# A rebuilt opening of a fused mLSTM-cell and tanh-shrink kernel: transfers, early gates, clock filling and the split of work between VectorE and ScalarE

## The chip, the core and the metric

The kernel runs on one core of a Trainium2 chip. The metric is the device time of one execution in microseconds (us). Before the change it is 556.27 us, the median of three runs (555.25 to 557.56).

## The reference, cut to what matters

Two blocks follow each other. The first is an mLSTM cell over 4 batches, 8 heads, 768 steps and head dimension 40; its output, turned to 3072 tokens by 320 features, goes through a two-layer MLP (320 to 2048 to 320).

```python
for t in range(S):
    m_new = np.maximum(f_gate[:, :, t] + m, i_gate[:, :, t])
    f_stab = np.exp(f_gate[:, :, t] + m - m_new)
    i_stab = np.exp(i_gate[:, :, t] - m_new)
    C = f_stab * C + i_stab * einsum('bhd,bhe->bhde', vt, kt)
    n = f_stab * n + i_stab * kt
    h_tilde = einsum('bhde,bhe->bhd', C, qt)
    denom = np.maximum(np.abs(einsum(n, qt)), 1.0)
    y[:, :, t] = sigmoid(o_gate[:, :, t]) * h_tilde / denom
x = y as (B*S, H*D)
h = x @ w_in
out = (h - np.tanh(h)) @ w_out
```

The inputs are float32; the two MLP matrices come in 64-bit floats, and the kernel makes its own float32 from their bits.

## The kernel before, in words

**Units.** The cell is cut into 24 units: chunk c of 128 steps, batch b, all 8 heads, unit n = 4c + b. For a unit TensorE (PE) forms the scores of queries and keys (`scores`, L555, tile `ps`), VectorE (DVE) masks them into `P` (L564) and scales v by the input gates into `vs` (`scaled`, L546), PE multiplies `P` with `vs` per head and, for c > 0, the carried state with the queries (`intra` L589, `inter` L580, tile `ph`), DVE forms the denominator `den`, multiplies the output gate `o` by it and the result `ys` by that (`gate`, L594), PE turns `ys` (`turn`, L623, tile `px`), and ScalarE (ACT) copies it to `xT`. The state is carried by `update` (L606, tile `pc`) and `keep_state` (L614). A float32 matmul stands in the trace as two passes.

**MLP.** Two units make a group of 256 tokens, and w_in and w_out are cut into 8 blocks p. A pair (group, p) is a first product (`up`, L751, tile `ph_up`), the shrink polynomial on ACT (`z`, `q`) and DVE (`gt`), and a second product (`down`, L806, tile `po`). The first four groups are done for p = 0, 1, 2, ... as the weights come (`RUNS`, L236). Each block is brought in by GpSimd's DMA queue (POOL) and turned from 64-bit to 32-bit floats by DVE and ACT: `parts` (two instructions), `low`, `power` (ACT), `one`, `sign`, `product` (`weights`, L450). The tiles are `w` (64-bit), `w_e`, `w_m`, `w_r`, and `w_in`, `w_out` as results.

**Gates.** `gate_rows` (L375) runs the recurrence of m along rows of 32 (batch, head); `gate_columns` (L394) turns the rows with PE, sums them with PE (`lfT` with `upto` and `ones`, tile `gate`), bounds and exponentiates them (`ei`, `inv`, `eT`). This is done in three passes, for chunk 0, chunk 1 and chunks 2 to 5 (`CHUNKS`, L365).

**What sets the order.** The first 12 units and the 32 pairs of the first four groups are planned at build time by the class `Plan` (L157): each step is put down with its engine, an assumed length, its predecessors, the buffers that it takes and gives, and a rank; `run` (L193) always takes the step that can start first, and issues its instructions. The result is a fixed list for each engine, executed in that order. The assumed lengths decide the order only. `idle` (L1099) puts matmuls of a tile of ones (`awake`, 128x512 in bf16) into stretches in which the plan leaves PE free. After the planned part (from the 32 pairs on) the order is interleaved by another piece of code.

**The opening.** Before the plan starts, the gate rows of chunks 0 and 1, `kz` of units 0 and 1 and both `o` are issued on SyncE's queue (SP), `qz` on ACT's, `v` on POOL's (L282, L316 to L321). ACT loads its table for exp when it has issued its four transfers. `qz` and `kz` hold every second head per half of the partitions, so that each of their transfers is 40 partitions of 4 pieces of 512 bytes.

Of the kernel before, what the change touches and what calls it, by code (L numbers as in the profile page):

```python
# [56 lines left out]
PSUM = bass.MemoryType.PSUM  # L57
NO_SYNC = mybir.DependencyInfo(mybir.DependencyClass.NoSync, mybir.DependencyReason.DATA)

L = 128  # L60
# [18 lines left out]
def kernel(  # L79
# [77 lines left out]
    class Plan:  # L157
# [5 lines left out]
        RATE, SHARED = 0.25, 32.4  # L163

        def __init__(self, **tokens):
            self.tokens = {name: [(0.0, tag) for tag in (range(tags) if isinstance(tags, int) else tags)] for name, tags in tokens.items()}
            self.turns = {name: 0 for name, tags in tokens.items() if isinstance(tags, int)}
            self.count = tokens
            self.todo, self.free, self.serial, self.moved = [], dict.fromkeys("TVASGN", 0.0), 0, dict(S=8.0, G=6.5)
            self.tiles = 1  # L170

        def add(self, engine, us, step, after=(), rank=0.0, take=(), give=(), at=0.0, kb=0.0, tiles=1, hold=0.0):
            self.serial += 1
            op = {"engine": engine, "us": us, "step": step, "after": list(after), "rank": rank, "serial": self.serial,
                  "take": take, "give": give, "at": at, "kb": kb, "tiles": tiles, "hold": hold, "end": None}
            self.todo.append(op)
            return op
# [15 lines left out]
        def run(self, idle):  # L193
            while self.todo:
                _, _, _, _, t, op = min(((t[1], op["engine"] == "T" and op["tiles"] != self.tiles == 2, op["rank"], op["serial"], t[0], op)
                                         for op in self.todo if (t := self.start(op)) is not None), key=lambda x: x[:4])
                self.todo.remove(op)
                for name, held in op["take"]:
                    token = self.token(name)
                    self.tokens[name].remove(token)  # L200
                    if name in self.turns:
                        self.turns[name] += 1
                    held[name] = token[1]
                if op["engine"] == "T":
                    idle(self.free["T"], t)
                    self.tiles = op["tiles"]
                op["step"]()
                op["end"] = self.free[op["engine"]] = t + op["us"]
# [69 lines left out]
    def load_gates(c0, c1):  # L278
        for to, part in ((f_sb, f_gate), (i_sb, i_gate)):
            nc.sync.dma_start(out=to[:, c0 * L:c1 * L], in_=part[:, c0 * L:c1 * L])  # L280

    load_gates(0, 2)  # L282
# [10 lines left out]
    def load_unit(n, names=("kz", "qz", "v", "k", "o", "q2"), queue=nc.sync):  # L293
        c, b = divmod(n, B)
        t = ld.setdefault(n, {})
        for name in names:
            if name in ("kz", "qz"):
                t[name] = load.tile([128, HH, L], FP, name=name, tag=name, bufs=3)
                for i in range(2):
                    src = kT if name == "kz" else qT  # L300
                    queue.dma_start(out=t[name][i * HALF:i * HALF + D], in_=src[b, c, :, slice(i, H, 2)])
# [14 lines left out]
    for n in range(2):  # L316
        load_unit(n, ("kz",))
        load_unit(n, ("qz",), A)
        load_unit(n, ("v",), G)
    for n in range(2):  # L320
        load_unit(n, ("o",))  # L321
# [5 lines left out]
    A.activation(out=probe, in_=probe, func=AF.Exp)  # L327
    ident = const.tile([128, 128], FP, name="ident")
# [6 lines left out]
    V.memset(diag, 1.0)  # L335
# [6 lines left out]
    V.memset(ones, 1.0)  # L342

# [5 lines left out]
                    pattern=[[1, 128]], channel_multiplier=-1)  # L349
    spare = []  # L350
# [14 lines left out]
    CHUNKS = (0, 1, 2, NT)  # L365
# [83 lines left out]

    def weights(dst, srcs, queue):  # L450
# [5 lines left out]
        def fetch():  # L456
# [3 lines left out]
            for rows, cols, part in srcs:  # L460
                queue.dma_start(out=to[rows, cols], in_=part)  # L461

        def parts():
# [4 lines left out]
            V.tensor_single_scalar(e, w["hi"], 0x7FF00000, op=OP.bitwise_and)  # L468
# [23 lines left out]
        return fetch, parts, low, power, one, sign, product  # L492

    def blocks_of(p):
# [4 lines left out]
        every, whole = slice(0, 128), [(slice(0, 128), slices(0, 2), moe_w_in[0:128, slices(2 * p, 2)])]  # L499
        for i in range(2):  # L500
            full, half = (FROM[2], FROM[1]), (FROM[1], FROM[2] + HALF)
            whole.append((every, slices(2 + i, 1), moe_w_in[full[i]:full[i] + 128, slices(2 * p + i, 1)]))
# [3 lines left out]
                        [(every, slice(i * DM, (i + 1) * DM), moe_w_out[slices(2 * p + i, 1), :]) for i in range(2)], nc.gpsimd))  # L506
# [29 lines left out]
    def prepare(n, whole=True):  # L536
# [4 lines left out]
        t["vs"] = scaled(n, 0, "vs", 4)  # L541
# [4 lines left out]
    def scaled(n, i, name, bufs):  # L546
# [5 lines left out]
        V.tensor_tensor(out=to[:, :, 0:D], in0=t["v"], in1=scale.unsqueeze(2).to_broadcast([L, H, D]), op=OP.mult)  # L552
# [36 lines left out]
    def intra(n, h):  # L589
        t = un[n]  # L590
        T.matmul(t["ph"][:, h, :], t["P"][:, h % 2, h // 2, :], t["vs"][:, h, :], start=(t["c"] == 0 and h == 0), stop=True,
                 skip_group_check=True)

    def gate(n):  # L594
# [4 lines left out]
        V.scalar_tensor_tensor(out=den, in0=ph[:, :, D], scalar=-1.0, in1=inv[:, t["c"], t["hs"]], op0=OP.mult, op1=OP.max)  # L599
        V.tensor_tensor(out=den, in0=den, in1=ph[:, :, D], op=OP.max)  # L600
        V.reciprocal(out=den, in_=den)
        V.tensor_tensor(out=sg, in0=sg, in1=den.unsqueeze(2).to_broadcast([L, H, D]), op=OP.mult)
        y = t["y"] = ys[n % 2]
        V.tensor_tensor(out=y.rearrange("p (h d) -> p h d", d=D), in0=ph[:, :, 0:D], in1=sg, op=OP.mult)
# [146 lines left out]
    def up(some, shrink):  # L751
# [4 lines left out]
        def product(i, x, j):  # L756
# [3 lines left out]
            if j < NK:  # L760
                lhs, rhs = w_in[:, p, (2 * j + i) * 128:(2 * j + i + 1) * 128], xT[g % NX][:, at, :]
# [110 lines left out]
    PLANNED = 12  # L872
# [60 lines left out]
    def plan_unit(n, rank):  # L933
# [10 lines left out]
        if n < 2:  # L944
            times = ((6.1, 3.6, 9.0), (7.6, 5.6, 10.5))[n]
            for name, at in zip(("qz", "v", "o"), times):
                u[name] = plan.add("N", 0.0, (lambda: arrive(n)) if name == "qz" else (lambda: None), at=at - 1.7)
        else:
            load("kz", 1.5, 164, (n - 3, "scores"))
            load("qz", 1.5, 164, (n - 3, "scores"))  # L950
            load("v", 0.5, 164, (n - 3, "prep"))
            if c:
                load("q2", 1.5, 164, (n - 3, "second"))
# [12 lines left out]
        u["scores"] = plan.add("T", 1.35, first_part, [u["qz"]], rank, [("a", held), ("P", held)], tiles=2, hold=HOLD * (n // B))  # L966
        u["mask"] = [plan.add("V", 0.68, lambda i=i: ready[1][i](), [u["scores"]], rank, give=[("a", held)] if i else ())
                     for i in range(2)]
        before = of(n - B, "state")
        u["prep"] = plan.add("V", 0.47, lambda: prepare(n, whole=False), [u["v"], u["scores"], *of_tokens[c]], rank, [("vs", held)])  # L970
        u["column"] = plan.add("A", 0.2, lambda: un[n]["column"](), [u["prep"]], rank - 0.2)
        u["open"] = plan.add("A", 0.47 if n else 1.75, lambda: open_gate(n), [u["o"], u["scores"], *of_states[0], *exponentials], rank - 0.1)
        op = None

        def second_part(j):
            banks[:] = [held["small"]]
            inter(n, j)
            for h in TRIOS[j]:
                intra(n, h)

        for j, heads in enumerate(TRIOS):
            op = plan.add("T", 0.145 * len(heads) + (0.14 if c else 0.0), lambda j=j: second_part(j), [op] if op else [*u["mask"], u["prep"], u["column"], *before, *of(n, "q2") * (c > 0)], rank,
                          take=() if op else [("small", held)], give=[("P", held)] if j == len(TRIOS) - 1 else ())
        u["second"] = op
        u["gate"] = plan.add("V", 1.5, lambda: gate(n), [op, u["open"], *of(n - 2, "turn")], rank, give=[("small", held)])
# [8 lines left out]
        def turns():  # L994
            banks[:] = [held_x["small"]]
            for j in range(NK + 1):
                turn(n, j, at_once=False)

        u["turn"] = plan.add("T", 0.35, turns, [u["gate"]], rank, [("small", held_x)])
        u["x"] = plan.add("A", 0.5, lambda: keep_x(n), [u["turn"]], rank, give=[("small", held_x)])  # L1000
        late = rank + (0.1 if c else 1.9)
        u["update"] = plan.add("T", 0.55, updates, [u["second"], u["k"]], late, [("small", held_c)], [("vs", held)],
                               at=0.0 if c else 24.0 if n < 2 else 40.0)
        u["state"] = plan.add("V", 1.0 if c else 0.5, lambda: keep_state(n), [u["update"], *before, *of_states[c]], late, give=[("small", held_c)])

    converted = {}

    def plan_weights(p, rank, at):
        for k, block in enumerate(blocks_of(p)):
            fetch, parts, low, power, one, sign, product = block  # L1010
            held, r, buffer = {}, rank + 0.36 * k, "w64" + "ab"[k]
            op = plan.add("S" if k else "G", 1.5 if k else 2.8, fetch, (), r, [(buffer, held)], at=(13.0 if p else 6.0) if k else at, kb=655)
            op = plan.add("V", 1.0, parts, [op], r, [("w", held)])
            two = [plan.add("A", 0.74, step, [op], r) for step in (low, power)]
            op = plan.add("V", 0.82, one, two[:1], r)
            op = plan.add("V", 0.82, sign, [op, two[1]], r, give=[(buffer, held)])
            converted[p, k] = plan.add("V", 0.82, product, [op] + (of_tokens[NT - 1] + of_states[NT - 1] if p >= KEPT else []), r, give=[("w", held)])

    plan.free["T"] = 2.1
    plan_gates(0, -2.0, 3.3, in_small)  # L1020
    plan_gates(1, -1.64, 3.3, in_po)
    for n in range(2):
        plan_unit(n, -1.0)
    plan_weights(0, 0.08, 3.0)
    for n in range(2, PLANNED):
        g = n // GT
        if n == 2 * B:
            plan_gates(2, 1.17, 30.0, in_po)
# [7 lines left out]
    def plan_item(x):  # L1036
# [24 lines left out]
        op = plan.add("T", 0.47 + 0.43 * n, rest, [op], rank, tiles=2)  # L1061
# [37 lines left out]
    def idle(t0, t1):  # L1099


        n = int((t1 - t0) * 0.9 / 0.43 if t0 < 6.0 else (t1 - t0) * 0.4 / 0.215)
        if n and not busy:
            awake(n)
        elif n and plan.tokens["a"] and plan.tokens["a"][0][0] <= t0:
            stream(ps_a.tile([128, 512], FP, name="awake", tag="a0"), n)

    plan.run(idle)


# [82 lines left out]
    def begin_any(n):  # L1193
# [3 lines left out]
        for i in range(2):  # L1197
            spread(t["P"][:, i], f_rows, n, slice(i, H, 2))
# [155 lines left out]
```

## Time and profile before

| | us |
|---|---|
| median of three runs | 556.27 |
| the profiled execution | 555.29 |
| its span, first to last instruction | 553.5 |
| PE busy | 538.0 (97%) |
| DVE busy | 346.2 (63%) |
| ACT busy | 182.8 (33%) |
| first `ph_up` matmul starts at | 27.44 |
| `px` of units 4, 5, 6, 7 starts at | 66.15, 76.30, 89.64, 99.92 |
| `px` of unit 11, the last planned one | 152.81 |

The profile's page gives the busy time of each engine, a picture of the span in 40 slices, the DMA queues, the chain of waits that ended last, and the costliest groups of instructions. The timeline view lists instructions in order of time and merges equal ones; "x16" are sixteen in a row. The window view gives the busy time per engine in chosen stretches. A busy PE isn't PE at its peak: `awake` matmuls count as busy, and so does a matmul that runs at half pace.

### The profile page before, as it was taken

The page shows a single profiled execution, that of the slowest core. Times are in us where ns is not written, and L with a number is a line of the kernel's source. Part 1 is how long each engine was busy: PE and PEld are TensorE (multiplying, and loading weights), DVE is VectorE, ACT ScalarE, POOL GpSimd, SP SyncE. Part 2 cuts the span into 40 slices and gives each one's busy share as a digit, 9 for nine tenths or more (in the row PEclk, how much of TensorE's full clock was granted, in tenths as well). Part 3 has the DMA queues.
Part 4 walks back from the last instruction along what each step waited for, and adds up shares of the span by engine and source line. Part 5 has one row for each costly group of instructions (what it writes and reads, how often), then busy time and mean ns, then how long its engine had stood idle before and what let it go on. Part 6 is the DMA issues. An engine that isn't in the chain of part 4 may idle for free.

```text
span 553.5 us, 8989 instructions
## 1 busy us (share of the span) xinstructions
PE 538.0 (97%) x3381; PEld 455.9 (82%) x3384; DVE 346.2 (63%) x754; ACT 182.8 (33%) x449; POOL 33.6 (6%) x67
## 2 busy tenths in 40 slices
PE   7998999999999999999999999999999999999995
PEld 5777788888877776798899999999989989988873
DVE  4699788989864335767656647547547547553421
ACT  3355734543342312322232242232233233232331
POOL 6142021400000000000000000000000000000000
PEclk9999999999999999999999999999999999999999
DMA  7798354633300001201202212112110000000000
GB/s 214 193 264 246 84 165 150 174 116 109 98 26 0 1 0 50 82 21 56 86 28 59 64 39 70 48 37 60 49 37 12 1 25 1 1 25 1 24 1 30
DMA packets 39819, 37.97 MB, mean 69 GB/s; under 512 B 3993, under 2 KB 37337, under 8 KB 39769
## 3 DMA queue, kind: packets, MB, share of 16 engines
q1 hardware_dynamic: 32336, 22.24, 14.5%
q0 software_dynamic: 3296, 10.82, 6.6%
q10 hardware_dynamic: 4136, 4.26, 2.2%
q8 instruction: 29, 0.48, 0.4%
q14 instruction: 22, 0.17, 0.1%
HBM read 33.37 MB, written 3.93 MB: 67 GB/s over the span
## 4 chain that ended last, share of the span: by engine, by line
PE 92%; DVE 3%; ACT 2%; DMA 1%; issue 1%; SPq 0%; DVEq 0%; ACTq 0%
PE ph_up L129 39%; PE pS L129 20%; PE po L129 15%; PE ph L129 9%; PE ps L129 4%; PE px L133 2%; PE pc L129 2%; DMA kz<-in_kT 1%; ACT L106 1%; DVE w_e L106 1%; DVE gt L106 1%; PE awake L129 0%; DVE P L106 0%; DVE w_in L106 0%; DVE w_r L106 0%
## 5 line engine op out<-in xcount | busy, mean ns | idle before, releaser
L129 PE MATMUL ph_up<-xT,w_in 128*128 128x256 f32 (+1 forms) x1152 | 245.9, 391 | 2.2 <-DVE w_in L106 1.1
L129 PEld LDWEIGHTS ph_up<-xT,w_in 128*128 128x128 f32 (+1 forms) x1152 | 169.4, 189 | 35.6 <-issue 13.5
L106 ACT ACTIVATE z<-ph_up 128x512 f32<-128x512 f32 (+1 forms) x100 | 57.1, 576 | 286.8 <-issue 155.6
L106 DVE SCALAR_TENSOR_TENSOR gt<-ph_up,z 128x512 f32<-128x512 f32 (+1 forms) x100 | 63.4, 663 | 92.7 <-ACT z L106 92.4
L129 PE MATMUL po<-w_out,gt 128*128 128x320 f32 x320 | 93.6, 438 | 0.8 <-ACT eT L106 0.8
L129 PEld LDWEIGHTS po<-w_out,gt 128*128 128x128 f32 x320 | 58.7, 190 | 26.1 <-issue 4.0
L106 DVE TENSOR_TENSOR P<-ps,upto 128x512 f32<-128x512 f32 x48 | 31.4, 683 | 67.5 <-PE ps L129 67.4
L106 ACT ACTIVATE q<-z,tiny 128x512 f32<-128x512 f32 (+1 forms) x100 | 64.9, 701 | 0.0
L129 PEld LDWEIGHTS ph<-vs,P 128*128 128x128 f32 x384 | 60.1, 202 | 5.7 <-issue 1.5
L106 DVE SCALAR_TENSOR_TENSOR gt<-q,gt 128x512 f32<-128x512 f32 (+1 forms) x100 | 63.1, 660 | 0.2 <-ACT q L106 0.2
L129 PE MATMUL ph<-vs,P 128*128 128x41 f32 x384 | 58.9, 273 | 0.0
L129 PE MATMUL pS<-wT,s 128*128 128x160 f32 x336 | 51.3, 300 | 0.0
L129 PEld LDWEIGHTS pS<-wT,s 128*128 128x128 f32 x336 | 47.3, 190 | 0.0
L129 PE MATMUL pS<-w_out,gt 128*128 128x160 f32 x224 | 40.4, 310 | 0.0
L129 PEld LDWEIGHTS pS<-w_out,gt 128*128 128x128 f32 x224 | 32.7, 194 | 1.3 <-issue 1.0
L129 PEld LDWEIGHTS ps<-qz,kz 40*128 40x128 f32 x384 | 27.6, 203 | 2.9 <-issue 1.2
L129 PE MATMUL ps<-qz,kz 40*128 40x128 f32 x384 | 29.1, 291 | 0.5 <-DMA kz<-in_kT 0.5
L461 POOL DMA_DIRECT2D w<-in_moe_w_in x40 | 21.7, 547 | 45.8 <-DVE w_e L106 22.3
L129 PE MATMUL ph<-state,q 120*128 120x123 f32 (+1 forms) x120 | 24.4, 284 | 0.0
L106 ACT COPY xT<-px 128x384 f32<-128x384 f32 x24 | 11.4, 474 | 33.8 <-PE px L133 33.8
L129 PEld LDWEIGHTS ph<-state,q 120*128 120x128 f32 (+1 forms) x120 | 20.0, 191 | 1.7 <-issue 0.2
L106 DVE TENSOR_TENSOR s<-gt 128x256 f32<-128x256 f32 x56 | 21.0, 416 | 0.0
(90 smaller groups left out, 445.1 us busy)
## 6 DMA issues: line engine op xcount, KB each, us to landing
w<-in_moe_w_out POOLq DMA_DIRECT2D x16, 320.0 KB, 5.2
kz<-in_kT SPq DMA_DIRECT2D x48, 80.0 KB
o<-in_o_gate SPq DMA_DIRECT2D x24, 160.0 KB
out<-ob ACTq DMA_DIRECT2D x24, 160.0 KB
k<-in_k SPq DMA_DIRECT2D x20, 180.0 KB
qz<-in_qT SPq DMA_DIRECT2D x44, 80.0 KB
v<-in_v SPq DMA_DIRECT2D x22, 160.0 KB
q<-in_qT SPq DMA_DIRECT2D x40, 60.0 KB
```

The lines of the kernel that those rows point to most:

```text
L106: i = method(*args, **kwargs)
L129: return cls.keep(nc.tensor.matmul(*args, **kwargs))
L133: return cls.keep(nc.tensor.transpose(*args, **kwargs))
L461: queue.dma_start(out=to[rows, cols], in_=part)
```

## The change

All of it lies in the opening and in the planned part.

- **Transfers.** The early ones are put in another order: `qz` of unit 0 (ACT queue), f gates, first half of `kz`, i gates, second half of `kz`; the rest of units 0 and 1 later, `v` of unit 0 on POOL between the memsets, `v` of unit 1 between two weight transfers, `o` on SP from within the plan. `qz` and `kz` now hold heads 0 to 3 and 4 to 7 per half, so that a transfer is 40 partitions of one piece of 2048 bytes. A block of weights has 4 and 1 transfers where it had 5 and 2, and the second block's first transfer waits for the first instruction that DVE runs on the first block.
- **Gates.** Chunks 0 and 1 are one pass, 256 columns wide.
- **Ones.** The tile for `awake` is set in two halves, so that its first half is ready sooner; the plan counts how dense PE's last 2.6 us were, and puts `awake` matmuls (or a dense step) before a sparse step where the share would fall under 0.48. `idle` fills 0.9 of a gap rather than 0.4, and may use any free PSUM bank.
- **ScalarE.** From unit 2 on to unit 11, the scaling of v and the product of `o` with `den` are done by ACT, head by head: 8 instructions of 128x40 each, in place of one DVE instruction of 128x320.
- **First units.** For c = 0 the product with `vs` is in two halves of four heads, each of which needs its half of the mask only.
- **Timing.** Assumed lengths, transfer rates and start times of the plan are set anew. `low` and so on are unchanged.

In program order the changed kernel has 48 `awake` matmuls (22 before), 33 of them ahead of the first `ph_up` (14 before). The tail of the PE list, from about the 32nd pair on, is the same in both.

```diff
-        RATE, SHARED = 0.25, 32.4
+        RATE, SHARED, COLD, TURN, WAIT = 0.3, 28.0, (7.0, 1.8), 0.12, 0.2
+        FEW, SPAN = 0.48, 2.6
...
+        def run(self, idle, fill):
...
+                if op["engine"] == "T":
+                    turn = self.TURN * (op["tiles"] != self.tiles)
+                    if t > self.COLD[0] and op["dense"] < 0.6 and self.share(t, op["us"], op["dense"]) < self.FEW:
+                        other = min(((x, o) for (x, _), o in ready if o["engine"] == "T" and o["dense"] >= 0.6 and x < t + 0.3),
+                                    key=lambda x: (x[1]["rank"], x[0], x[1]["serial"]), default=None)
+                        if other:
+                            t, op = other
+                        else:
+                            free = self.free["T"]
+                            n = fill(free, t + 0.3)
...
-                    queue.dma_start(out=t[name][i * HALF:i * HALF + D], in_=src[b, c, :, slice(i, H, 2)])
+                    queue.dma_start(out=t[name][i * HALF:i * HALF + D], in_=src[b, c, :, i * HH:(i + 1) * HH])
...
-    for n in range(2):
-        load_unit(n, ("kz",))
-        load_unit(n, ("qz",), A)
-        load_unit(n, ("v",), G)
-    for n in range(2):
-        load_unit(n, ("o",))
+    load_unit(0, ("qz",), A)
+    load_gates(0, 2, ((f_sb, f_gate),))
+    load_unit(0, ("kz",), between=lambda: load_gates(0, 2, ((i_sb, i_gate),)))
...
+    load_unit(1, ("kz",))
+    load_unit(1, ("qz",), A)
...
-    V.memset(diag, 1.0)
+    V.memset(diag[:, 0:HH], 1.0)
...
+    V.memset(diag[:, HH:H], 1.0)
...
-    CHUNKS = (0, 1, 2, NT)
+    CHUNKS = (0, 2, NT)
...
+                i = queue.dma_start(out=view, in_=part)
+                if behind:
+                    tc.add_manual_dep(i.ins, behind[-1].ins.name, SYNC, reason="order of transfers")
...
+        if by_heads:
+            for h in range(H):
+                A.mul(out=to[:, h, 0:D], in_=t["v"][:, h], mul=scale[:, h:h + 1])
+        else:
+            V.tensor_tensor(out=to[:, :, 0:D], in0=t["v"], in1=scale.unsqueeze(2).to_broadcast([L, H, D]), op=OP.mult)
...
+        def shares():
+            for h in range(H):
+                A.mul(out=sg[:, h], in_=sg[:, h], mul=den[:, h:h + 1])
...
-    PLANNED = 12
+    PLANNED, SHARED = 12, 2
...
+        shared = n >= SHARED
+        u["prep"] = plan.add("A" if shared else "V", 1.0 if shared else 0.45, lambda: prepare(n, whole=False, by_heads=shared), [u["v"], u["scores"], *of_tokens[c]], rank, [("vs", held)])
...
+        parts = TRIOS if c else [range(i * HH, (i + 1) * HH) for i in range(2)]
...
+        if shared:
+            steps = []
+            over = plan.add("V", 0.6, lambda: [steps.extend(gate(n, in_parts=True)), steps[0]()], [op], rank)
+            shares = plan.add("A", 1.0, lambda: steps[1](), [over, u["open"]], rank)
+            u["gate"] = plan.add("V", 0.5, lambda: steps[2](), [shares, *of(n - 2, "turn")], rank, give=[("small", held)])
...
-        n = int((t1 - t0) * 0.9 / 0.43 if t0 < 6.0 else (t1 - t0) * 0.4 / 0.215)
+        one = 0.43 if t0 < plan.COLD[0] else 0.217
+        n = int((t1 - t0) * share / one)
```

## The prediction

> **What bounds the kernel now.** First the busy tenths of the page, then the window view.
>
> ```profile
> PE   7998999999999999999999999999999999999995
> DVE  4699788989864335767656647547547547553421
> ...
> DMA  7798354633300001201202212112110000000000
> ```
>
> ```profile
> 0.00:27.40 27.40, 22.93 (x111) 17.53 (x112) 16.25 (x51) 10.14 (x29) 11.45 (x28) 1.00 0.76 204
> 27.40:62.50 35.10, 31.54 (x209) 25.07 (x212) 31.51 (x67) 20.19 (x46) 9.60 (x17) 1.00 0.78 217
> 62.50:153.00 90.50, 90.50 (x600) 75.21 (x600) 79.37 (x162) 38.26 (x86) 12.59 (x23) 1.00 0.46 133
> ```
>
> Columns: stretch, length, then busy PE, weight loads, DVE, ACT, POOL, clock, DMA share, GB/s. From 62.5 us on PE is never idle: nothing outside it can shorten that part, and the change leaves its work there alone. Whatever is to be gained lies before. There PE looks 84 to 90% busy, but the PE timeline shows what it is busy with:
>
> ```profile
> 13.71 3.63 PE L129 MATMUL ph<-vs,P 128*128 128x41 f32 x16
> 17.56 0.63 PE L129 MATMUL awake<-diag 128*128 128x512 bf16 x1 [0.22 <-issue]
> 17.99 3.47 PE L129 MATMUL ph<-vs,P 128*128 128x41 f32 x16
> ...
> 24.17 1.67 PE L129 MATMUL ps<-qz,kz 40*128 40x128 f32 x16
> 25.77 0.82 PE L129 MATMUL awake<-diag 128*128 128x512 bf16 x3
> 27.44 0.45 PE L129 MATMUL ph_up<-xT,w_in 128*128 128x256 f32 x1 [0.85 <-DVE w_in L106]
> ```
>
> The same 16 `ph` passes take 1.98 us at 29.96. So PE runs at half pace until about 25 us. I price every pass at its pace in the dense part (start to start: `ph_up` 0.216, its 64-row form 0.158, `po` 0.269, `ph` 0.111, `ps` 0.062, `px` 0.109, `pc` 0.105) and call the rest of the time waste; an `awake` is waste. Up to the first `ph_up` PE has done 8.2 us of work in 27.44: waste 19.2. Up to `px` of unit 4 (66.15) 40.2: waste 26.0. Up to that of unit 11 (152.81) 125.2: waste 27.6. After that nothing changes. So at most some 20 us can be had, and 19.2 of the waste lie ahead of the first `ph_up`. Between 27 and 62.5 the rate is set by DVE: 31.5 busy of 35.1. Its largest gap there (3.1 us at 56 to 59) waits for ACT:
>
> ```profile
> 53.22 1.28 ACT L106 ACT_TABLE_LOAD   x1
> 54.51 0.28 ACT L106 ACTIVATE ei<-gate 128x128 f32<-128x128 f32 x1
> 54.81 1.28 ACT L106 ACT_TABLE_LOAD   x1
> 56.10 0.47 ACT L106 ACTIVATE o<-o 128x320 f32<-128x320 f32 x1
> 56.59 1.28 ACT L106 ACT_TABLE_LOAD   x1
> ```
>
> [...] half pace after 2.3 us of `awake` at 2.09, and through 7.5 us of `ph`; full pace after 3.2 us of `awake`, `px` and `ps` from 21.9 (the clock column says 1.00 throughout and doesn't show it). [...] `q` has a pointer bias and goes at 613 ns per 512 columns and 399 per 256, start to start, which gives 185 + 0.84 per column. [...] the second half of `kz` of unit 0, issued by 3.5, is waited for until 8.1.
>
> **The change, part by part, on the way to the first `ph_up`.** (1) Transfers. Only gates (64 KB), `qz` and `kz` of unit 0 (328 KB) go ahead: 392 KB at the 208 GB/s measured from 2 to 6 us land at 3.9 us, with some sharing 4.7. The pieces of 2048 bytes:
>
> ```profile
> q1 hardware_dynamic: 32336, 22.24, 14.5%
> ...
> q10 hardware_dynamic: 4136, 4.26, 2.2%
> ```
>
> q1 has 688 bytes per packet and moves 22.24 MB in 14.5% of 16 x 553.5 us, 17.3 GB/s per engine; q10, with 1030, moves 21.9. So 0 to 25% faster; I take 0. Their issue (0.77 us) falls to about 0.35, the price of the other SP transfers; off the path. i gates are now behind one `kz` half: recurrence starts at 3.6 rather than 3.22. Moved transfers: `o` goes behind `kz` of unit 1 on SP and is needed after ACT's second table load at about 11; `v` of unit 1 goes behind four weight transfers on POOL (0.55 each) and is needed at 12; both are issued by 6, and 2.6 MB in all are wanted by 13, which the 204 to 290 GB/s of the first 16 us carry. Cost nothing, 1 us if they come late. The new wait on POOL (weights p = 1 behind DVE's first `w_e` of p = 0): all later weight transfers queue behind it, and DVE's parts of `w_in` 1 wait for them, in the new list some 9 us later; 655 KB need 3 at 217 GB/s: nothing, and 3 us without that cover. (2) PE warms: first half of the ones at 1.6 us, seven `awake` at 0.427 to 4.65, `ps` of unit 0 (2.1 at half pace) to 6.8, turned gates to 7.4. By then 5 us were busy: warm at 7 [...] else within the ten `awake` that follow `ps` of unit 1. (3) One gate pass: 256 columns lie between the 128 (1.28 us to `lf`) and the 512 (3.0): 1.85, `lf` at 5.5. DVE then masks half of `ps`, copies `lfT` 7.6; sums by 8.2, bounded 8.6, `eT` and `inv` on ACT to 9.5, `ei` 9.7, one mask 0.6, `vs` 0.4: 10.8. The second pass that falls away (about 1.9 us of DVE, 1.2 of ACT) lay where DVE was idle in part. (4) PE (for c = 0 in halves of four heads, which start one mask, 0.6, earlier): `ps` of unit 1 to 9.4, ten `awake` at 0.217 to 11.5, `ph` of unit 0 to 13.3. DVE: gate of unit 0 (0.2 + 0.2 + 0.24 + 0.52 + 0.41 = 1.57) to 14.9; `w_r` 0.74, mask 0.6, sign 0.74, parts 0.8, gate of unit 1 1.57, product 0.73: `w_in` at 20.1. `px` of unit 1, copy to `xT` 0.48 and three `awake`: first `ph_up` at 20.7; I take 21.0. With 8.7 us of work ahead of it in the new order the waste is 12.3 instead of 19.2: **6.9 gained**.
>
> (5) From there to `px` of unit 4 the new PE list has 28.8 us of work and 14 `awake` (3.0), the new DVE list 31.7. Both are full, so they get in each other's way: 1.0 us (0 to 3). Waste 4.0 instead of 6.8: **2.8**. In this are DVE's relief, `vs` 0.40 + `o` 0.52 for units 2 to 4 (10 units in all: 9.2), and one table load less in the ACT list at the third gate pass (1.28). (6) After `px` of unit 4 DVE has 67.5 us for 72.7 of PE, before 75.4 for 85.0, since the new list takes units earlier: tighter, waste 2.1 instead of 1.6: **-0.5**.
>
> (7) The pieces on ACT. No row shows such an instruction. From below: `vs` columns (128x8, no pointer) 0.10 start to start plus 32 columns is 0.126, so 1.0 for eight, what the plan reckons with. From above: the `q` line at 40 columns, 0.219, so 1.75 for eight. I take 1.75, since the scale is a pointer. That is 0.75 later, twice per unit. Between `den` and `ys` DVE has other work in its list: unit 2 two masks and `w_r` (1.9), unit 3 `w_r` and a gate row (1.3), unit 4 mask, sum and state (1.95), later 1.4 to 1.7. So `ys` is late by 0 to 0.5; PE has dense pairs between for most of it. I charge 0.2 per unit, 10 units: **-2.0**, with 0 and -15 as ends. ACT itself has room: 38.3 of 90.5 busy, 84 of 105 in the new list.
>
> Sum: 6.9 + 2.8 - 0.5 - 2.0 = 7.2. The profiled run's own time is 555.29 (span 553.5 and 1.8 around it): 548.1. The median lies 1.0 above the profiled run: **549.0**.
>
> **Rivals.** *All of it comes* (25%): the pieces go at 0.126 and the clock is up at 7: no charge for (7) and no mutual wait in (5), so 10.2 gained, 546. For it: `eT` pieces of 12 columns start 0.06 apart. Against: they have no pointer. *The start stays late* (20%): `kz` lands at 8 as now[...]; then gates, `ps` and `ph` shift by 3, and the first `ph_up` is at 24: 4.2 gained, 552. For it: DMA share is over 1.0 in 8 to 18 us. Against: 392 KB are ahead of it, where some 880 were. *The pieces bite* (10%): at 0.22 each all 1.5 us per unit are passed on, `den` to ACT to `ys` to `px` to `xT`, in an order that leaves no room: 15 lost against 9.2, 562, slower. It decides from 0.92 us per unit on. For it: DVE and PE lists are both full, and DVE waits in order. Against: ACT is 42% busy, and PE has other pairs queued. My forecast has 45%.
>
> **How the numbers follow.** The likeliest gives 549.0, from 547 to 552; with the rivals, 544.5 to 553.5 leaves out the slower one, and some of the late start. About 0.5%, 2.8 us, can be told from no change, so 553.5 is the bound. Faster: forecast 43, all 25, late 11: 0.79. Same: forecast 2, late 9, pieces 3: 0.14. Slower: 0.07.
>
> **What would show it.** First `ph_up` at 21 (24: late start); `ph` of unit 0 at 1.8 per 16 passes (3.6: cold); ACT's pieces start to start (0.126 or 0.22); DVE's idle ahead of `ys`, and PE's ahead of `px`; `px` of unit 11 at 127 (its work is 110.2 in the new order: waste 17). If that waste is over 28, I am wrong altogether; if it is 12, the charge of (7) was none.

## The result and the profile after

The changed kernel takes 552.98 us (median of 11 runs, 551.36 to 556.61) against 556.34 before (11 runs, 555.25 to 557.74): ratio 0.9944, 95% interval 0.9919 to 0.9970. In two later sets of runs the same kernel had 0.9932 (0.9914 to 0.9949) and 0.9932 (0.9910 to 0.9954). By the medians it is faster by 3.4, 3.9 and 4.6 us (by the three ratios 3.1 to 3.8), where 7.2 were forecast. Its profiled execution took 551.47 us, span 549.7.

The busy tenths of the page, TensorE (PE), VectorE (DVE) and DMA, look much as before:

```profile
PE   8999999999999999999999999999999999999995
DVE  4789899998243426767755656647546547553411
...
DMA  7987465533000002211211211111110000000000
```

The window view, cut at the new first `ph_up` and at `px` of units 4 and 11 (columns as in the prediction):

```profile
0.00:26.32 26.32, 23.40 (x136) 15.53 (x136) 15.79 (x44) 11.52 (x31) 10.79 (x25) 1.00 0.85 245
26.32:60.20 33.88, 33.22 (x232) 26.83 (x233) 30.13 (x66) 27.97 (x92) 6.24 (x10) 1.00 0.73 224
60.20:134.74 74.54, 74.54 (x511) 61.96 (x510) 68.38 (x137) 58.35 (x183) 9.90 (x16) 1.00 0.50 151
```

Counted with the prediction's prices per pass, PE does 9.1, 28.7 and 72.6 us of work in these stretches. What is left of each stretch is waste:

| stretch | before | forecast | after | gained, forecast | gained |
|---|---|---|---|---|---|
| to the first `ph_up` (before 27.44, forecast 21.0, after 26.32) | 19.2 | 12.3 | 17.2 | 6.9 | 2.0 |
| from there to `px` of unit 4 | 6.8 | 4.0 | 5.2 | 2.8 | 1.6 |
| from there to `px` of unit 11 | 1.6 | 4.1 | 1.9 | -2.5 | -0.3 |

The gains sum to 3.3 us, most of the 3.8 by which the profiled time fell. The largest error lies ahead of the first `ph_up`, 4.9 us; 2.2 us of it came back in the third row. The timeline of PE there:

```profile
4.66 0.79 PE L130 MATMUL ps<-qz,kz 40*128 40x128 f32 x2
6.62 2.04 PE L130 MATMUL ps<-qz,kz 40*128 40x128 f32 x14 [1.17 <-DMA kz<-in_kT]
...
10.85 2.08 PE L130 MATMUL ps<-qz,kz 40*128 40x128 f32 x16
12.86 3.84 PE L130 MATMUL awake<-diag 128*128 128x512 bf16 x10
16.53 1.88 PE L130 MATMUL ph<-vs,P 128*128 128x41 f32 x16
...
25.07 0.49 PE L134 MATMUL px<-ident,ys 128*128 128x128 f32 x3
...
26.32 0.89 PE L130 MATMUL ph_up<-xT,w_in 128*128 128x256 f32 x3
```

The ten `awake` take 3.67 us from their start to that of `ph`, 0.427 each until 15.9 us. That is half pace, held 9 us longer than forecast. VectorE (DVE) has `vs` of unit 0 ready at 14.05, but its `ph` starts at 16.53, behind the `awake`. From 15.9 on the pace is full (`ph` x16 in 1.8 us, before 3.6).

The next lines show ScalarE (ACT) around the last gate pass. Before, three table loads stood there in 5 us; the two at 45.46 and 54.17 are left:

```profile
45.46 1.28 ACT L107 ACT_TABLE_LOAD   x1
...
53.85 0.30 ACT L107 ACTIVATE inv<-inv 128x128 f32<-128x128 f32 x1
54.17 1.28 ACT L107 ACT_TABLE_LOAD   x1
55.46 0.47 ACT L107 ACTIVATE o<-o 128x320 f32<-128x320 f32 x1
55.84 1.84 ACT L107 ACTIVATE vs<-v,ei 128x40 f32<-128x40 f32 x8
```

Eight pieces take 1.75 us (`vs` starts at 55.84, the next instruction at 57.59): 0.219 each, as the prediction took them. Queue q1 moves the same 22.24 MB in fewer and longer packets and a smaller share of time: 14.5% of 553.5 us were 80 us, 13.7% of 549.7 are 75, 6% less:

```profile
q1 hardware_dynamic: 21296, 22.24, 13.7%
```

### The profile page after: what moved, and what is told of

Same layout as the page of the kernel before. It is cut to its first block, busy times and chain, and to the rows that moved or that the text cites. A ratio compares the mean times of both kernels' runs of the same rounds, so it can differ in the third digit from the quotient of the medians.

```text
span 549.7 us, 9137 instructions
## 1 busy us (share of the span) xinstructions
PE 539.5 (98%) x3406; PEld 454.0 (83%) x3406; DVE 335.4 (61%) x726; ACT 214.5 (39%) x600; POOL 26.9 (5%) x51
## 3 DMA queue, kind: packets, MB, share of 16 engines
q1 hardware_dynamic: 21296, 22.24, 13.7%
## 4 chain that ended last, share of the span: by engine, by line
PE 90%; DVE 1%; DMA 1%; ACT 0%; issue 0%; ACTq 0%
PE ph_up L130 40%; PE pS L130 20%; PE po L130 16%; PE ph L130 8%; PE ps L130 3%; PE pc L130 2%; PE px L134 2%; DMA w<-in_moe_w_in 1%; ACT o L107 0%; PE awake L130 0%; DVE P L107 0%; DVE wT L107 0%; DVE gt L107 0%; PE gate L134 0%; DVE ys L107 0%
## 5 line engine op out<-in xcount | busy, mean ns | idle before, releaser
L130 PEld LDWEIGHTS po<-w_out,gt 128*128 128x128 f32 x320 | 58.5, 190 | 25.4 <-issue 5.5
L130 PEld LDWEIGHTS ph<-vs,P 128*128 128x128 f32 x384 | 57.2, 191 | 5.6 <-ACT vs L107 0.6
L130 PE MATMUL ph<-vs,P 128*128 128x41 f32 x384 | 55.7, 261 | 0.1
L130 PEld LDWEIGHTS ps<-qz,kz 40*128 40x128 f32 x384 | 26.8, 199 | 3.4 <-issue 1.4
L130 PE MATMUL pS<-wT,gt 128*128 128x160 f32 x112 | 20.7, 302 | 0.0
L492 POOL DMA_DIRECT2D w<-in_moe_w_in x32 | 18.7, 590 | 35.5 <-DVE w_e L107 15.5
```

The source lines that it names most:

```text
L130: return cls.keep(nc.tensor.matmul(*args, **kwargs))
L492: i = queue.dma_start(out=view, in_=part)
```

## The experiments

The head is all that lies ahead of the first `ph_up`. Two theories say why it is late. **A**, the clock: PE stays at half pace, and falls back to it. **B**, the transfers: `kz` and the i gates landed at 6.6 and 4.45 us instead of 4.7 and 3.6. **C** and **D** say what the pieces on ACT are worth. Later theories (E to H) are in the expectations. The stretches of half and full pace are read from the distance of equal matmuls (`awake` 0.427 or 0.216, `ph` 0.216 or 0.111, `ps` 0.13 or 0.07). From the first change to full pace on, the clock column of the window view has them too, as 0.50 or 1.00 (e1 has 0.50 from 22 to 24 us); up to then it reads 1.00 although the passes go at half pace (the changed kernel from 4 to 14 us, with `awake` at 0.427). The changed kernel's 552.3 to 553.0 is the measure; all ratios are to the kernel before on the same chip.

**e1_fill** (median 552.91 us, ratio 0.9947, interval 0.9929 to 0.9964). All other instructions stay in their order.

```diff
-            awake(n)
+            awake(n + (5 if t0 < 2.0 else 0))
```

> Five more multiplications without use (awake) at the very start of TensorE, nothing else. Theory A (the clock): TensorE stays at half pace until 15.9 us because its first seven awakes end at 5.45 us and leave a gap to 6.62. With twelve of them, about 2.1 us longer, the gap is closed, full pace comes at about 8 us, the ten awakes behind ps of unit 1 take 2.1 instead of 3.7 us, ph of unit 0 starts at 14.3 instead of 16.5, the first ph_up at 24.1 instead of 26.3: 2.2 us faster than the changed kernel, about 550.8. Theory B (the transfers): what holds the head is kz and the i gates, which the fill doesn't move: 553.0, the first ph_up within 0.5 us of 26.3.

The clock did as A said, even earlier; the time didn't. Full pace came at 4.9 us, `ph` of unit 0 at 13.24 instead of 16.53, the first `px` 3.3 us earlier; but the first `ph_up` came at 26.12 (after: 26.32). The timeline of PE shows where the 3.3 us went:

```profile
17.09 0.53 PE L134 MATMUL px<-ident,ys 128*128 128x128 f32 x3
...
18.91 1.03 PE L130 MATMUL awake<-diag 128*128 128x512 bf16 x4
21.42 1.43 PE L130 MATMUL ph<-vs,P 128*128 128x41 f32 x8 [1.48 <-ACT vs L107]
22.65 1.91 PE L130 MATMUL awake<-diag 128*128 128x512 bf16 x4
24.35 0.84 PE L134 MATMUL px<-ident,ys 128*128 128x128 f32 x3
```

PE came to `ph` of unit 2 before its `v` had landed (ACT began `vs` at 19.41, after 1.28 us of waiting for that transfer), stood 1.48 us, and fell back to half pace at 22.0 (`awake` 0.427 again at 22.65). `px` of unit 1, whose `ys` was done at 21.3, stood behind all that in the fixed list.

**e2_v_later** (553.70, 0.9953, 0.9935 to 0.9971) and **e3_v_later_fill** (554.47, 0.9951, 0.9932 to 0.9971), the second with the edit of e1 as well.

```diff
-    load_unit(0, ("v",), G)
...
-                u["v"] = plan.add("N", 0.0, lambda: None, at=7.0 - 1.7)
+                u["v"] = plan.add("G", 0.6, lambda: [load_unit(n, ("v",), G), arrive(n)], at=3.5, rank=-1.0, kb=164)
...
+            if t0 == 0:
+                begun.append(i)
```

> GpSimd's transfers moved behind the first gate scan: v of unit 0 and the first weights are issued after it instead of from 1.6 us. Theory B (the transfers): over half of the DMA from 2.6 to 6 us goes to these transfers, so without them the i gates land at about 3.5 instead of 4.45 us and the second half of kz at about 4.7 instead of 6.62; the gate chain is 1 us earlier, ps of unit 0 ends near 7 instead of 8.5, TensorE is warm earlier too, and the first ph_up starts 1.5 to 4 us earlier (22.3 to 24.8): 549 to 551.5. Theory A alone: the i gates come earlier but the awakes at half pace hold ph of unit 0: under 1 us gained, 552 to 553. Against both: v or the weights come too late and the first ph_up is later than 26.3: 553.5 or more.

> Both edits together. If the two causes are separate the gains add: 2.2 for the clock and 1.2 for the transfers, first ph_up near 22.9, 549.6. If they are one cause (kz late leaves the gap, the gap leaves the clock low), the sum is no more than the larger of the two alone.

B's first link failed: the i gates were there at 5.51 and 5.26 us, no earlier than in the three profiles of the changed kernel (4.45, 5.74 and 6.08), though in e2 GpSimd's queue had moved 0.16 MB from 2 to 6 us instead of the 0.42 of the first of them. There was no gain. In e3 full pace held from 5.1 to 15.3 us, and half pace from there to 32.4; the first `ph_up` came at 29.27.

**e6_same_again** (552.34, 0.9932) and **e14_same_third** (552.25, 0.9932), the changed kernel with no edit.

> The changed kernel once more, nothing edited. If the state of TensorE's pace is set by the code alone, the pace turns to full at 15.8 us again and not down again, and the first ph_up starts at 26.3 within 0.3. [...] the turn to full pace and a turn back to half fall elsewhere, by 3 us or more, and the first ph_up moves with them. The time: 552.98 within 1.

> The changed kernel a third time, nothing edited, as the measure for the one before. 552.3 to 553.0. In the profile the stretches of half and full pace fall differently again, with the first ph_up between 25.5 and 31 (the kernel with earlier gates alone, which has the same order on TensorE, once had it at 31.6).

Of the two outcomes the second came: this is one list of instructions in three profiles, and the turns fall elsewhere in each. In the first, full pace came at 15.9 us. In e6 it came at 5.5, was lost at 8.95 and came back at 15.8; in e14 it came at 5.2, was lost at 8.65 and came back at 15.5. The timeline of e6 shows it in the `ps` of units 0 and 1:

```profile
6.89 1.13 PE L130 MATMUL ps<-qz,kz 40*128 40x128 f32 x14 [1.44 <-DMA kz<-in_kT]
...
9.85 2.08 PE L130 MATMUL ps<-qz,kz 40*128 40x128 f32 x16
11.86 4.25 PE L130 MATMUL awake<-diag 128*128 128x512 bf16 x10
```

The first `ph_up` came at 26.32, 25.73 and 25.36. In both repeats the early full pace was lost before the ten `awake`. The spread of 25.5 to 31 that was expected of e14 showed only in e9, below.

**e7_fill_px_first** (554.28, 0.9951, 0.9932 to 0.9969): the edit of e1, and

```diff
+        if n == 2:
+            before = [*before, units[1]["turn"]]
```

> The five more awakes at the start, and ph of unit 2 has to come behind px of unit 1 (with the fill alone, px of unit 1 stood behind ph of unit 2, whose vs waited for v, and started 2.6 us after its ys). Theory A: the first ph_up starts at 22.5 to 23.5 and what is won there is kept: 549 to 550.5. Theory E (the stretch to 60 us is bound by VectorE and ScalarE, which make the weights): the first ph_up starts at 22.5 to 23.5 but the fifth px stays at 60 to 61 and the time at 552 to 553.5.

In its profile PE stood 1.84 us at 9.3 (behind DVE's `ei`), full pace was gone from 12.1 to 15.5, and the first `ph_up` came at 25.39. A second thing showed in DVE's waits from 26 to 46 us, in this kernel and, smaller, in the changed kernel, e1 and e2:

```profile
DVE w_in L107 <- DMA w_out<-in_i_gate: 4.6, 1, 4.6
```

and in its timeline:

```profile
35.34 0.48 DVE L107 TENSOR_SCALAR w_m<-w 128x640 int32<-128x640 int32 x1
40.40 1.27 DVE L107 TENSOR_TENSOR_SCAN w_in<-w_out,w_in 32x512 f32<-32x512 f32 x1 [4.58 <-DMA w_out<-in_i_gate]
...
44.89 0.49 DVE L107 TENSOR_TENSOR ys<-ph,o 128x320 f32<-128x320 f32 x1 [0.64 <-ACT o L107]
```

The last gate pass waits in DVE's queue for a transfer that SyncE issued at 35.19, and `ys` of unit 3 stands behind it; PE waited 3.9 us for it and lost its pace. The wait was 1.3, 1.2 and 2.1 us in the three profiles of the changed kernel and 2.6 in e1. Theory G, that this wait takes back what the head wins, came from this.

**e8_no_awakes** (556.61, 0.9998, 0.9983 to 1.0014).

```diff
         if n and not busy:
-            awake(n)
+            pass
```

> The 33 multiplications without use ahead of the first ph_up are left out, the order of all else is kept. Theory A (they bring and hold full pace): everything ahead of the first ph_up stays at half pace; ph and ps of three units are some 11 us of TensorE at half pace instead of 5.5 at full, and the first ph_up starts 2 to 4 us later: 555 to 557. Rival F (they only stand in the way of ph of unit 0, 3.7 us of them): first ph_up at 23 to 26, 552 or less.

The whole gain is gone, so the `awake` ahead of the first `ph_up` are needed for it, though the loss is not where A put it. The timeline of PE:

```profile
13.15 3.61 PE L130 MATMUL ph<-vs,P 128*128 128x41 f32 x16 [1.27 <-DVE vs L107]
...
26.91 2.07 PE L130 MATMUL ph_up<-xT,w_in 128*128 128x256 f32 x4 [0.57 <-ACT xT L107]
28.77 1.76 PE L130 MATMUL ph<-vs,P 128*128 128x41 f32 x8
30.47 2.08 PE L130 MATMUL ps<-qz,kz 40*128 40x128 f32 x16
```

`ph` of unit 0 starts 3.4 us earlier without the ten `awake`, then goes at half pace, and the first `ph_up` starts at 26.91, 0.6 later than in the changed kernel. But half pace lasts to 38.0 us, and from the first `ph_up` to `px` of unit 4 the waste is 9.7 instead of 5.2. The runs lie within 2.0 us of each other (555.76 to 557.75); in its three sets those of the changed kernel spread over 5.2 to 6.3.

**e9_gates_earlier** (550.92, 7 runs, 0.9909, 0.9875 to 0.9943). Only SyncE's order changes.

```diff
-... load_gates(c0, c1), (), rank - 0.5, at=at - 4.0, kb=33 * (c1 - c0))]
+... load_gates(c0, c1), (), rank - 3.0, at=at - 14.0, kb=33 * (c1 - c0))]
```

> The gates of the second pass (1 MB before 128 KB of them are waited for at 36 to 40 us) are issued some 8 us earlier on SP, the order on all other engines stays. In the runs so far VectorE stood 1.2 to 1.3 us (changed kernel), 2.6 us (fill) and 4.6 us (fill and px first) for i_gate, in front of den and ys of unit 3. Theory G (this wait takes back what the head wins): it goes, the fourth px starts 1 us earlier, 551.3 to 552.0. Rival: what is behind it on SP (v, qz, q2 of units 4 and 5) comes later instead and takes its place: 552.3 to 554.

The wait is gone: in its profile the scan, at 41.87, waits for nothing. The median is 0.4 below G's range, though the interval overlaps that of the changed kernel. Five of the runs lie at 550.35 to 551.19, two at 556.1 and 556.5. The profile fell on one of these two:

```profile
16.87 2.15 PE L130 MATMUL ph<-vs,P 128*128 128x41 f32 x16
18.95 1.16 PE L130 MATMUL ps<-qz,kz 40*128 40x128 f32 x16
20.05 1.22 PE L130 MATMUL ph<-vs,P 128*128 128x41 f32 x8
21.06 0.88 PE L134 MATMUL px<-ident,ys 128*128 128x128 f32 x3
22.16 1.06 PE L130 MATMUL awake<-diag 128*128 128x512 bf16 x2 [0.22 <-DVE P L107]
...
31.56 1.10 PE L130 MATMUL ph_up<-xT,w_in 128*128 128x256 f32 x4
```

PE has the order of the changed kernel and is never idle for over 0.22 us here, yet `px` at 21.06 goes at half pace (0.88 us for three, in e13 0.53): full pace came at 17.4, was lost at 20.9 after `ph` and `ps` passes alone (128x41 and 40x128), and came back at 31.1. The first `ph_up` is 5.2 us later than in the first profile of the changed kernel, the time 4.6 later.

**e10_fill_px_gates** (550.06, 6 runs, 0.9906, 0.9871 to 0.9941) and **e13_best_again** (550.34, 6 runs, 0.9895, 0.9868 to 0.9922): the edits of e1, e7 and e9 together, twice.

> Five more awakes at the start, ph of unit 2 behind px of unit 1, gates of the second pass earlier. Theory A and G: with the wait for i_gate gone (4.6 us in front of ys of unit 3 with the first two edits alone) the fourth px is at 42 or before and the time falls from 554.3 to 550 to 551.5. If other transfers are the limit instead, the fourth px stays later than 44 and the time over 553.

> The kernel with the fill, px of unit 1 first and the earlier gates once more, nothing edited, beside the changed kernel on the same chip. If its gain of 2 to 3 us on the changed kernel is its own and not luck of a few runs: 549.5 to 551.5. If it came from runs in which the pace held: 552 or more, and the profile shows half pace somewhere from 8 to 30 us.

In the two profiles full pace came at 4.8 and 4.6 us and was kept to over 540. PE's timeline of e13:

```profile
3.67 2.14 PE L130 MATMUL awake<-diag 128*128 128x512 bf16 x7
5.74 1.71 PE L130 MATMUL ps<-qz,kz 40*128 40x128 f32 x16
...
10.21 2.11 PE L130 MATMUL awake<-diag 128*128 128x512 bf16 x9 [0.16 <-issue]
12.15 1.88 PE L130 MATMUL ph<-vs,P 128*128 128x41 f32 x16
...
23.54 1.13 PE L130 MATMUL ph_up<-xT,w_in 128*128 128x256 f32 x4 [0.67 <-ACT xT L107]
```

and DVE's, with the scan of the last gate pass not waiting any more:

```profile
5.54 0.68 DVE L107 TENSOR_TENSOR_SCAN w_in<-w_out 32x256 f32<-32x256 f32 x1 [3.34 <-DMA w_out<-in_i_gate]
...
10.86 0.48 DVE L107 TENSOR_TENSOR vs<-v,ei 128x320 f32<-128x320 f32 x1
...
34.09 1.27 DVE L107 TENSOR_TENSOR_SCAN w_in<-w_out,w_in 32x512 f32<-32x512 f32 x1
```

In e10 the first `ph_up` is at 22.47. The order of e7 puts 8 `ph` passes more ahead of it, so the work there is 10.0 us and the waste 12.5, against 12.3 forecast: once full pace held and `px` of unit 1 no longer stood behind `ph` of unit 2, the head wasted what the prediction had said. In e13 the first `ph_up` is at 23.54. In the two profiles `px` of unit 4 is at 57.6 and 57.7 (after: 60.2), and the profiled times are 549.51 and 549.13. This is the fastest version. Beside e14 on the same chip it is 1.9 us faster by the medians; the two intervals overlap a little (0.9868 to 0.9922 and 0.9910 to 0.9954), so the size of this last step is known only roughly. Nor is it shown how much of it the pace brings: e9, with the earlier gates alone, has 0.9909 on the chip on which e10 has 0.9906.

**e11_awakes_moved** (552.46, 7 runs, 0.9923, 0.9896 to 0.9950): e10, with eight of the ten `awake` moved ahead of `ps` of unit 1. The minus line is that of the changed kernel.

```diff
+            if n == 1:
+                awake(8)
...
-            awake(n)
+            awake(2 if 9.9 < t0 < 10.3 and n > 8 else n + (5 if t0 < 2.0 else 0))
```

> As the one before, and eight of the ten awakes that stood behind ps of unit 1 stand ahead of it. Theory A: full pace, reached at 5 us with the fill, was lost again when TensorE had only a few passes to run from 8 to 11 us; with the awakes there it holds, ph of unit 0 starts at 13.2 at full pace in most runs, the first ph_up at 22.5 to 23.5 (ph of unit 0 and 9.5 us), and the time is 548.5 to 550.5, with less spread between runs. If the pace falls all the same, as the kernel before it.

It didn't hold the pace: full from 6.3 to 16.5, then half to 26.8, with the first `ph_up` at 28.27.

**e4_no_act_pieces** (556.99, 1.0012, 0.9996 to 1.0027) and **e15_best_no_pieces** (556.51, 0.9997, 0.9983 to 1.0011, on top of e13).

```diff
-    PLANNED, SHARED = 12, 2
+    PLANNED, SHARED = 12, 12
```

> The scaling of v and the gate stay on VectorE as in the kernel before; the rest of the changed kernel is kept and the order is planned anew for it. Theory A and B: the pieces cost little and win little, the head decides: 551.5 to 554.5, the waste from the fifth px on about as in the kernel before (1.6 us). Rival C (the pieces bite): 2 us or more faster than the changed kernel, 551 or less. Rival D (the pieces pay): VectorE is late in the stretch to unit 5, where the changed kernel wastes 1.7 us less than the kernel before: 555 or more.

> The kernel of e13 with the scaling of v and the gate on VectorE. Theory C (the pieces pay by what they take off VectorE, whatever the pace): 3 to 5 us slower than e13, 553 to 555.5, and VectorE has over 95% from 20 to 55 us also where TensorE goes at full pace. Rival H (in the changed kernel without pieces it was the pace, lost from 20.5 to 27.4 us, that cost the 4 us): within 1.5 us of e13.

Without the pieces 4.5 and 6.2 us are lost (against 552.3 to 553.0 and 550.34): e4 fell out as its rival D said, and H (that the pace alone cost e4 its time) is out as it was put. But DVE isn't full in e15 (27.2 of the 35 us from 20 to 55, 78%; 82% from 20 to 31.3, while PE is at full pace), so C's reason is wrong too, and its 3 to 5 us were too few. DVE's timeline in e15:

```profile
25.06 1.29 DVE L107 TENSOR_TENSOR P<-ps,upto 128x512 f32<-128x512 f32 x2
28.22 0.49 DVE L107 TENSOR_TENSOR vs<-v,ei 128x320 f32<-128x320 f32 x1 [1.87 <-DMA v<-in_v]
...
37.65 0.17 DVE L107 SCALAR_TENSOR_TENSOR den<-ph,inv 128x8 f32<-128x8 f32 x1 [3.34 <-PE ph L130]
```

The first `ph_up` is at 22.84, between those of e10 and e13. Then a `v` is late: DVE stands with all its queue for 1.87 us, and PE for 1.76 at 27.8. PE's pace is half from 31.3 to 41.5, and DVE waits 3.34 us for `ph`. The waste from the first `ph_up` to `px` of unit 4 is 12.8 (e13: 5.2). In e13 DVE waits for no `v`: ACT reads it. The plan also puts unit 4 elsewhere without the pieces (`px` at 69.3), and how much of the 6.2 us is this, the late `v` or the pace isn't separated.

**e12_act_only** (558.43, 1.0033, 1.0022 to 1.0045): the kernel before, with the pieces of the diff in it, planned at 1.75 us per eight where the changed kernel plans 1.0. An earlier form, e5, planned them at 1.0 and gave no result.

```diff
+        shared = n >= 2
-        u["prep"] = plan.add("V", 0.47, lambda: prepare(n, whole=False), [...
+        u["prep"] = plan.add("A" if shared else "V", 1.75 if shared else 0.47, lambda: prepare(n, whole=False, by_heads=shared), [...
```

> The kernel before with one part of the change alone: from unit 2 on the scaling of v and of the gate go to ScalarE in eight pieces, at the 1.75 us per eight that the trace shows; the head stays as it was and the order is planned with these steps. The changed kernel without the pieces was no faster than the kernel before (556.99 to 556.52). Theory C (the pieces are the gain): VectorE is relieved by some 8 us, and this kernel is 2.5 to 4.5 us faster than the kernel before: 552 to 554. Rival D (the pieces pay only together with the new head and its schedule): within 1.5 us of 556.5, or slower.

It is slower by 2.0 us. Full pace came at 30.4 instead of 25.3, and the waste from the first `ph_up` to `px` of unit 4 was 10.2 instead of 6.8. Which of the two led to the other wasn't separated. The rival D of this run holds in its stronger form: taking the pieces out of the changed kernel costs 4.5 us, and putting them into the old one costs 2.0.

**e16_before_awakes** (561.99, 6 runs, 1.0079, 1.0055 to 1.0103): the kernel before.

```diff
-        n = int((t1 - t0) * 0.9 / 0.43 if t0 < 6.0 else (t1 - t0) * 0.4 / 0.215)
+        n = int((t1 - t0) * 0.9 / (0.43 if t0 < 7.0 else 0.217))
```

> The kernel before with one thing of the changed one: TensorE's planned idle time ahead of the first ph_up is filled with 90% instead of 40% of multiplications without use (56 instead of 22 in the first part of its list). Theory A (the pace is what the head was short of): full pace comes before 20 us instead of at 25 and the time falls by 2 to 4 us, 552.5 to 554.5. Against it (the rest of the old head, transfers and two gate passes, sets the start): within 1.5 us of 556.4.

The opposite of A's number. PE's timeline:

```profile
15.29 3.63 PE L129 MATMUL ph<-vs,P 128*128 128x41 f32 x16
19.15 1.91 PE L129 MATMUL awake<-diag 128*128 128x512 bf16 x4 [0.22 <-issue]
20.86 3.47 PE L129 MATMUL ph<-vs,P 128*128 128x41 f32 x16
24.12 0.88 PE L133 MATMUL px<-ident,ys 128*128 128x128 f32 x3
24.80 3.62 PE L129 MATMUL awake<-diag 128*128 128x512 bf16 x8
```

The ones start at 2.1 us here, five in a row, and go on in fours. They cost 0.427 each where the plan reckons 0.217, and full pace comes only at 28.6 us, behind eight in a row. The first `ph_up` moves from 27.44 to 32.16.

## Why the prediction was right in direction and wrong in size

The direction and the range held; the size didn't. By its steps:

- **(1) Transfers.** Issue took 0.28 to 0.39 us as estimated, and the new wait of the weights costs DVE nothing. The i gates and `kz` missed by 0.9 and 1.9 us in the first profile (2.5 and 2.2 in e6). That mattered little: in e13 the i gates were there at 5.54, later than in the first profile, and `vs` of unit 0 began at 10.86, where the prediction had it end at 10.8, since `ps` and the gate sums went at full pace. (From 2 to 16 us the view of before reads 208 to 334 GB/s, not 204 to 290; nothing hangs on it.)
- **(2) PE warms: this step failed.** The prediction named two cases, "warm at 7" and "else within the ten `awake`", and put the first into the sum. In the first profile the second came true, at 15.9. In e6 and e14 PE was at full pace at 7, as in the first case, but lost it at 8.95 and 8.65, before the ten `awake`. So two things were wrong: the good case was taken for certain, and full pace was taken to stay. The trace of before could have warned: there 7.5 us of `ph` from 13.71 had kept PE busy and not brought full pace; yet the prediction counted `ps` passes among its "5 us busy", and that these would bring it at 7 was its author's estimate.
- **(3) One gate pass.** From scan to `lf` it took 1.9 us (forecast 1.85). `lfT` came at 9.05 instead of 7.6, since DVE stood 2.02 us for `ps`, which began late behind `kz` and then ran at half pace.
- **(4)** `ph` of unit 0 was forecast for 11.5 and came at 16.53. The 9.5 us from there to the first `ph_up` were about right (9.8; 9.4 in e10, 11.4 in e13, where PE waited for `qz` and `xT`). With full pace `ph` is at 13.24 (e1, the fill alone), 13.1 (e10) and 12.2 (e13). So, read from single profiles, 3.3 to 4.4 of the 5 us are the pace. For the last 2.5 us before its start `ph` was ready and stood behind the ten `awake`: all were priced at 0.217, and seven of them took 0.427.
- **(5)** The gain was 1.6 instead of 2.8. The scan's wait for the i gates, 1.3 us, was not in the prediction. It was 2.6 and 4.6 us in the faster starts of e1 and e7, which took back a part of what they had won.
- **(6), (7)** The change was -0.3 instead of -2.5. The price of a piece was right to the third digit, the charge too high: `ys` waits for ACT 0.06, 0.65, 0.32 and 0.47 us in units 2 to 5. The worth of the pieces was also booked in the wrong place. The prediction gave the head 6.9, and the pieces a charge of 2.0 beside a relief of DVE that is part of the 2.8 of (5). Measured, the changed kernel without the pieces gains nothing (1.0012), the pieces in the old kernel lose 2.0 us, and both together gain 3.4 to 4.6. The parts don't add, so measuring them one by one would not have given the whole either.

The sum and the sign disagree in the prediction itself: 27.6 of waste less 7.2 is 20.4 up to `px` of unit 11, which puts it at 130.6, not at 127 with a waste of 17. Measured, it came at 134.74 with a waste of 24.3.

That the time still fell into the range is in part luck: the pieces cost 2.2 us less than charged, against 4.9 lost in the head. The same holds for the rival "the start stays late": its 552 is within 1 us of the median, but `kz` was there at 6.62 us instead of its 8, and the first `ph_up` came at 26.32, 2 us later than its 24. The three profiles of the changed kernel have the first full pace at 15.9, 5.5 and 5.2 us; the prediction took one value.

What stays open: what brings full pace and what keeps it; how much of the time the pace alone is worth, since e1 and e7 brought full pace early and no gain, and e10 and e13 have the earlier gates too; and how much of the pieces' 4.5 to 6.2 us is the late `v` on DVE, how much the pace and how much the other order of the plan.

## What to carry to other kernels

Full pace had a price at both ends here. It came ahead of the useful work, at 4.6 to 7.4 us, in the seven profiles with twelve fill matmuls in a row from 1.6 us on, while in e16, with five from 2.1 us on and fours after them, it came only at 28.6. And each fill matmul that ran at half pace in front of ready work took 0.427 us instead of 0.216. Price a head at both paces, and treat a forecast that needs the good one as a chance. When a head gets faster, look for the next transfer that an engine's fixed list waits for: here 128 KB of gates, awaited at 36 to 40 us, took back a part of what was won at 13.

## What the runs showed of the hardware

- By the clock column of the window view, half pace began and ended at 22.0 and 25.4 us in e1, at 8.4 and 15.3 in e2, at 15.3 and 32.4 in e3 and at 20.5 and 27.4 in e4. These stretches of 3.4, 6.8, 17.1 and 6.8 us are about one, two, five and two times 3.4. Where they fall differs from profile to profile.
- Full pace was lost without PE being idle for more than 0.22 us, on 128x41 and 40x128 passes alone (e9 at 20.9 us); the same order of instructions on PE kept it there in the three profiles of the changed kernel, from 15.9, 15.8 and 15.5 us on.
- Idle times of 0.84 us (e3), 1.48 (e1) and 1.84 (e7) among such passes were each followed by half pace within 1.2 us. One of 0.74 among such passes in e13, and one of 1.4 in front of `pc` in e10, were not.
- The first i gates had landed by 4.45 to 6.08 us in the profiles with the new order of transfers, and no earlier in e2 and e3 (5.51 and 5.26), though in e2 GpSimd's queue moved 0.16 MB from 2 to 6 us, and in the first profile of the changed kernel 0.42.
